# One ring of eight PSUM banks in place of three rings, and a new hand-fixed order of all items, in a delta-rule attention with a softplus MLP behind it

## The chip, the cores and the metric

The kernel runs on one core of a Trainium2 chip. The metric is the device time of one launch in microseconds (us); lower is better. Engines are named as the profile names them: PE (TensorE matmul), PEld (its weight load), DVE (VectorE), ACT (ScalarE), POOL (GpSimd) and SP (SyncE, here only a queue that issues DMAs).

## The reference

Batch 4, 8 heads, 768 steps, head size 48. Each of the 32 heads runs a delta rule over time; the rows of all heads are then the input of a two-layer MLP with softplus.

```
k_n = k / (norm(k) + 1e-6);  state = 0            # per head, 48 x 48
for t in range(768):
    y[t]  = g[t] * (q[t] @ state)
    state = state + beta[t] * outer(k_n[t], v[t] - k_n[t] @ state)
x = y, as 3072 tokens x 384
out = softplus(x @ w_in) @ w_out                  # 384 -> 2048 -> 384
```

Inputs and output are float32; the kernel computes its matmuls in float16 with float32 sums.

## The kernel before

Time is cut into 12 chunks of 64 steps. Per chunk the recurrence is turned into matrices: normed keys and queries are transposed on PE (`trs`, lines 422 and 454), their products are formed (`gram`, line 516) and copied out of PSUM with a sign (`kkc`) or a triangular mask (`mask`), and for each **pair of chunks** the inverse of a unit triangular matrix is built by forward substitution: 15 `step` items, each two small elementwise instructions (lines 664 and 671) on DVE or POOL, then `ca`/`cb` (masked copies), `st` (transposes on DVE) and the matmuls `xmm`, `tmm`, `zmm` (lines 744, 768, 789). Pair 0 is chunks 0 and 1, pair 1 is chunks 2 and 3, and so on.

The serial part is a **chain** per chunk: `ks` (keys times state, line 826), `w` (DVE), `umm` (880), `u1` (a copy out of PSUM), `zu` (893), `u2` (copy), `smm` (910), `s` (new state, DVE), which starts the next chunk's `ks`. Beside it `qs` (826 too) and `ymm` (936) make the output, `y` multiplies by g on DVE, `ytr` (963) transposes, and `xt` copies the result out.

The **dense** part takes `xt`: chunks 0, 1, 10 and 11 alone, the others in pairs. `g1` (line 989) is the first layer, one PSUM bank of 512 columns per item; `soft` (1001, ACT) applies softplus into one of 16 `ga` buffers; `g2` (1016) is the second layer in quarters of 4 matmuls, summed over four quarters in one bank; `o` copies the bank out and two `store` DMAs send it off. `dense` matmuls use the whole 128 x 128 array, `trs` and `ytr` too; all other matmuls are packed as tiles of 64 x 64 or smaller. `fill` items (line 1046) are matmuls whose result nobody reads; they run where the order has nothing else for PE.

Everything is recorded as numbered items, 1286 of them, and emitted in the order of the table `_ORDER`: a letter for the engine (P, A, D, G for POOL, S for SP) and the item's number. Each engine runs its own items in that order and waits only where data or a buffer demands it. An item that needs a new buffer takes the one that was given back longest ago in its ring:

```
for b in it.bufs:
    if b.ap is None:
        b.slot = b.ring.free.pop(0)
...
    b.users -= 1
    if b.users == 0:
        b.ring.free.append(b.slot)
```

So the table sets the order on each engine and which instruction must have read a bank before PE may write it again. In PSUM the rings are `p_d` (5 banks, everything of the recurrence), `p_h` (2 banks, `g1` and `fill`) and `p_o` (1 bank, `g2`). The inputs k, q, v and g come by 96 loads of 192 KB from SP into a ring of 12 buffers; `w_in` and `w_out` come in four pieces each from POOL's queue (`wload`, line 330).

Of the kernel before, what the change touches and what calls it, by code (L numbers as in the profile page):

```python
# [10 lines left out]
F32 = mybir.dt.float32  # L11
# [76 lines left out]
def kernel(  # L88
# [13 lines left out]
    P = 128  # L102
# [8 lines left out]
    G8 = C // 8  # L111
# [9 lines left out]
    def ring(name, n, shape, dt, where=pool):  # L121
        return Ring([where.tile(shape, dt, name=f"{name}{i}") for i in range(n)], name)
# [949 lines left out]
D244 D245 D248 D246 A293 D250 S23 S42 G273 A368 P369 S57 A370 S66 P145 P194 P136 P255 A247 A249 S31
S58 S17 D196 P264 D251 D195 S18 D257 A254 D256 G253 P258 A300 G8 D252 G121 D265 A260 P301 P135 G123
D294 S20 D266 S19 D274 G6 A259 P261 P716 A13 A295 A262 A263 A717 A718 P191 D192 A275 S21 P719 A720
S38 S37 D193 D302 D721 P147 A713 G122 D16 P219 S65 G315 G14 G361 G126 P725 D221 G125 D220 P722 D727
D726 G316 P728 D296 P137 D276 D297 D277 A724 A723 A729 P934 P928 A935 A929 D362 G363 P298 D299 P926
A927 S40 P278 D279 P303 A304 P308 A310 A309 P930 D306 D305 P283 A284 A285 P936 D307 D312 D364 P288
A931 D311 G365 D287 D292 P731 P932 A289 A290 A937 S39 D291 D286 D313 G124 P366 P267 A268 A269 G730
P150 P270 S67 S45 A933 D314 G317 G318 D733 A381 G319 G320 A367 D732 S46 D382 P735 A737 A736 D272
D271 P949 P950 D321 D322 G127 G323 P222 D224 P734 S68 D223 D324 D325 S73 P738 P938 A739 A740 P744  # L1080
A939 D326 D745 P940 G327 P371 P741 D746 D328 P747 G128 P164 S81 D742 A748 G329 A372 S99 D743 A941
G330 P951 D374 P970 A373 D331 P376 A388 P956 A971 G332 D379 D380 P749 D375 S74 G333 A378 D334 P958
A377 A957 D751 G383 A959 D336 P964 D338 A337 P389 S82 A335 P962 A390 D339 G342 P952 A965 S48 P343
D384 P352 S76 A341 D345 D344 G385 A953 D750 D340 P960 P346 A449 A348 S84 P942 A961 S47 A963 D347
D354 P753 A754 P349 A469 S75 P966 D450 D351 G451 A350 D755 D353 P968 S83 A967 P386 D470 S100 S98
D387 P752 P756 D758 P943 D757 G471 S53 D452 P391 A393 S54 P944 D392 A954 D395 P762 D394 D764 P396
A397 A955 P759 D760 A398 P945 D761 A946 D401 S97 P355 P972 G403 G453 A356 A969 P454 G476 S55 A357
P973 D763 A455 S56 P765 D402 G404 G405 D400 P974 A766 D399 G406 P767 A456 P358 D769 P975 G407 A360
D768 G408 P457 D359 A976 A978 S977 P770 G409 D458 G410 P771 A772 P979 S105 D773 A557 P477 D411 P774
G412 D775 A776 S62 P980 A564 D472 P780 S61 G413 A478 P777 D781 P981 D782 G414 A947 D473 P783 A784  # L1090
P459 P982 D460 D461 P992 A983 D462 D778 P474 S64 A993 P1008 D558 S92 A475 P1000 D779 A1009 P464 S89
D463 P479 A1001 P986 D468 A481 S113 D482 A466 D483 P990 D480 G415 G491 G416 G417 G418 G419 A987 D465
G420 P785 A991 D467 P988 D786 D787 P1012 G421 A989 S71 P484 G559 D424 A423 P998 S114 D422 A1013 D488
S90 D426 P1025 A485 A425 P996 P440 A486 D427 A999 P431 A997 S70 P994 G579 P1002 G645 S91 D489 A995
G430 P1004 A1003 S80 D433 A429 P1026 D432 G492 A1005 D490 G493 G494 P434 S106 A985 D428 S63 P1006
A436 A435 P1014 G495 D441 A1007 D442 P437 A1015 P789 S948 G496 G497 D438 P1010 A537 D790 D487 P1016
A439 D791 A1011 P1027 G498 D538 S69 A1017 P788 D560 P1028 G539 D499 P792 A1029 D500 P565 A793 D794
P1018 A566 D501 P795 D797 A1031 P798 P1019 G502 A1030 D800 D799 A625 P443 G561 P1020 D796 A444 D540
A445 G503 P801 P1021 D646 G504 P446 A1022 P803 D448 P1032 A802 S1024 G505 G506 D447 S72 D804 P562
S94 D805 P1033 A563 D626 P807 A809 D808 A544 P806 S79 P1034 G507 P810 P1035 A811 S115 D508 D509 D512  # L1100
A812 D511 P545 A1036 P816 A546 D510 P813 S78 D817 P1039 S107 G541 A513 D818 P572 A573 D815 P819 D576
S77 P1040 G647 A820 D575 D514 P542 A574 P1048 A543 P1060 D814 D580 A1049 D515 P547 P567 A1061 P1066
D551 A568 D550 G517 A569 D570 P1068 A1067 G518 S1037 D549 P552 G627 P1062 A1069 A548 S116 P1058 D556
D571 D554 D553 S85 A1063 D577 D578 P821 A1038 P519 P1052 A1059 P1072 S108 A1053 S86 S112 S96 P1041
A1073 P1056 A1057 D581 P1064 S87 G582 D521 G583 G584 P1042 D823 D822 A1065 P1050 D520 G585 D516
P1046 G586 A1051 P522 P528 D555 P1054 A523 D529 A524 A1047 D587 D628 P525 P825 A1043 S1045 D530 S95
P1074 D526 D588 G589 A826 P1085 S1044 A1055 P531 A527 P824 P1070 D827 D533 G590 G591 A1075 D532 D667
A632 P828 A829 P1076 D830 A1023 P1086 G592 A1077 P831 A1071 P834 D833 G629 G668 G593 P1087 D835 D836
# [24 lines left out]
"""

# [28 lines left out]
```

## Time and profile before

| | |
|---|---|
| time of three runs | 243.43, 243.91 (median), 245.13 us |
| span of the profiled execution | 241.5 us |
| what lies around the span | the page gives no other time for the profiled execution; the runs are 1.9 to 3.6 us above its span, the median 2.4 us |
| PE busy | 219.4 us (91%), 5020 matmuls |
| DVE, ACT, POOL busy | 161.7 us, 152.8 us, 113.7 us |
| first dense matmul | 40.51 us |
| first dense matmul of chunks 2 and 3 | 89.77 us |
| end of the last matmul | 237.56 us |

A row of the timeline reads: start, duration, engine, line, operation, written tile<-read tiles, shape, count, and in brackets the idle time before and what ended it. Durations of matmuls overlap, since they are pipelined; what a group costs PE is the distance from its start to the start of the next group. A row of the windows reads: from:to, length, then busy time and number of instructions of each engine, the granted PE clock (1.00 is full), and DMA share.

### The profile page before, as it was taken

How to read it: one execution, taken by the hardware profiler on the slowest of the kernel's cores; microseconds unless marked ns; L12 is line 12 of the kernel's file. 1: busy time of each engine (PE TensorE's matmuls, PEld its weight loads, DVE VectorE, ACT ScalarE, POOL GpSimd, SP SyncE). 2: the span in 40 equal slices, each digit the busy share in tenths (PEclk: the TensorE clock that was granted, in tenths of full speed). 3: DMA queues.
4: the chain of work that ended last, by engine and by line, in shares of the span. 5: the costliest groups of instructions: out<-in, count | busy, mean ns of one | idle time of the engine just before them, and what ended most of it. 6: DMA issues, size and time to landing. Idle time of an engine off the chain costs nothing.

```text
span 241.5 us, 11396 instructions
## 1 busy us (share of the span) xinstructions
PE 219.4 (91%) x5020; PEld 135.6 (56%) x5020; DVE 161.7 (67%) x368; ACT 152.8 (63%) x292; POOL 113.7 (47%) x197
## 2 busy tenths in 40 slices
PE   7645877879988999999999999999999999999983
PEld 2423455646764664556655566655565555677751
DVE  2768699888897889987899757896496310623000
ACT  5767576764982778876895767757363674143540
POOL 8740393875779778989597482016620000000000
PEclk9985599999999999999999999999999999999999
DMA  6999989999999399961889514962302311303112
GB/s 102 182 245 137 167 135 190 176 173 180 180 217 167 57 177 164 162 113 35 150 153 184 97 30 94 160 122 52 69 21 52 68 34 25 64 19 81 35 33 65
DMA packets 86833, 27.57 MB, mean 114 GB/s; under 512 B 77048, under 2 KB 86776, under 8 KB 86784
## 3 DMA queue, kind: packets, MB, share of 16 engines
q1 hardware_dynamic: 80624, 20.83, 52.6%
q0 software_dynamic: 3840, 3.17, 8.5%
q10 hardware_dynamic: 2320, 2.85, 5.2%
q8 instruction: 39, 0.64, 1.2%
q14 instruction: 10, 0.08, 0.1%
HBM read 25.26 MB, written 4.72 MB: 124 GB/s over the span
## 4 chain that ended last, share of the span: by engine, by line
PE 75%; DMA 7%; DVE 6%; SPq 4%; issue 3%; ACT 2%; POOL 1%; DVEq 0%; ACTq 0%; POOLq 0%
PE o L1016 27%; PE h L989 26%; DMA w_in<-in_moe_w_in_dram 4%; PE d L826 3%; SPq L305 3%; PE d L936 3%; PE d L516 2%; DMA f<-in_q_dram 2%; PE d L422 2%; PE d L963 2%; PE d L454 2%; PE d L880 2%; PE d L910 2%; PE d L893 2%; PE d L768 1%
## 5 line engine op out<-in xcount | busy, mean ns | idle before, releaser
L1016 PE MATMUL o<-w_out,ga 128*128 128x384 f16 x384 | 77.7, 327 | 0.7 <-ACT osb L209 0.6
L1001 ACT ACTIVATE ga<-h 128x512 f16<-128x512 f32 x96 | 56.5, 599 | 29.8 <-PE h L989 25.9
L989 PE MATMUL h<-xt,w_in 128*128 128x512 f16 (+1 forms) x384 | 74.0, 327 | 0.5 <-DMA w_in<-in_moe_w_in_dram 0.3
L989 PEld LDWEIGHTS <-w_in 128*128 128x128 f16 x384 | 34.5, 98 | 21.2 <-DMA w_in<-in_moe_w_in_dram 0.8
L1016 PEld LDWEIGHTS <-ga 128*128 128x128 f16 x384 | 33.7, 98 | 21.8 <-issue 0.8
L664 POOL TENSOR_TENSOR tmp<-nn,tt 128x78 f32<-128x78 f32 (+7 forms) x53 | 19.2, 362 | 16.1 <-DVE tt L671 13.0
L373 POOL TENSOR_TENSOR nv<-nv,half_c 128x16 f32<-128x16 f32 x8 | 23.5, 2940 | 6.6 <-DVE nv L362 6.5
L671 POOL TENSOR_TENSOR tt<-tt,tmp 128x78 f32<-128x78 f32 (+7 forms) x53 | 20.4, 385 | 4.2
L498 DVE TENSOR_TENSOR mt<-d,mask 128x256 f16<-128x256 f32 x48 | 18.2, 413 | 4.5 <-PE d L516 3.5
L209 ACT ACTIVATE kqt<-d 128x1024 f16<-128x1024 f16 (+1 forms) x18 | 18.0, 1000 | 4.8 <-PE d L454 3.6
L211 DVE CAST u<-d 128x384 f16<-128x384 f32 x20 | 10.9, 554 | 14.3 <-PE d L880 7.9
L209 ACT ACTIVATE u<-d 128x384 f16<-128x384 f32 x28 | 13.0, 490 | 11.8 <-PE d L880 5.4
L1046 PE MATMUL h<-ident 128*128 128x512 f16 x52 | 18.1, 493 | 1.7 <-DVE ident L197 1.7
L209 ACT ACTIVATE kk<-d 128x256 f16<-128x256 f32 x37 | 13.4, 386 | 6.3 <-PE d L516 5.4
L209 ACT ACTIVATE osb<-o 128x384 f32<-128x384 f32 x19 | 9.3, 492 | 9.4 <-PE o L1016 9.3
L454 PE MATMUL d<-ident,qn 128*128 128x128 f16 x96 | 8.5, 243 | 6.7 <-ACT qn L209 5.9
L950 DVE TENSOR_TENSOR yg<-d,f 128x384 f16<-128x384 f32 x24 | 12.3, 551 | 2.9 <-PE d L936 2.8
L924 DVE TENSOR_TENSOR s<-s,d 128x384 f16<-128x384 f16 x20 | 10.4, 542 | 5.7 <-PE d L910 4.3
L644 POOL TENSOR_TENSOR nn<-ln,beta_l 128x256 f32<-128x256 f16 x8 | 6.1, 780 | 14.2 <-DVE ln L627 14.2
L209 ACT ACTIVATE xt<-d 128x768 f16<-128x768 f16 x10 | 8.1, 813 | 7.0 <-PE d L963 7.0
L866 DVE TENSOR_TENSOR w<-f,d 128x384 f16<-128x384 f32 x22 | 11.3, 545 | 1.4 <-ACT xt L209 0.7
L362 DVE TENSOR_REDUCE nv<-f 128x16 f32<-128x768 f32 x12 | 11.3, 942 | 1.0 <-ACT f L351 1.0
(117 smaller groups left out, 346.7 us busy)
## 6 DMA issues: line engine op xcount, KB each, us to landing
f<-in_k_dram SPq DMA_DIRECT2D x24, 192.0 KB, 5.7
f<-in_q_dram SPq DMA_DIRECT2D x24, 192.0 KB, 5.6
f<-in_v_dram SPq DMA_DIRECT2D x24, 192.0 KB, 5.3
f<-in_g_dram SPq DMA_DIRECT2D x24, 192.0 KB, 5.3
out_dram<-osb ACTq DMA_DIRECT2D x29, 96.0 KB, 2.7
out_dram<-osb SPq DMA_DIRECT2D x19, 96.0 KB, 2.8
w_in<-in_moe_w_in_dram POOLq DMA_DIRECT2D x4, 384.0 KB, 7.9
w_out<-in_moe_w_out_dram POOLq DMA_DIRECT2D x4, 384.0 KB, 8.4
```

What stands on the lines that cost most here:

```text
L209: nc.scalar.activation(o, x, AF.Copy, scale=float(sign))
L362: lambda en: nc.vector.tensor_reduce(nvs().rearrange("p (a h) -> p a h", a=2), ksq.ap, mybir.AxisListType.X, ALU.add),
L373: nc.gpsimd.tensor_tensor(nvs(), nvs(), half_c[:, :NU], ALU.pow)
L454: nc.tensor.transpose(o[:, j], qn.ap[:, j].rearrange("p m d -> p (m d)"), ident)
L498: nc.vector.tensor_tensor(mt[c][m].ap[:, NP * p : NP * p + NP], gb[m].ap.rearrange("p (i b) -> p i b", i=NP)[:, :, n : n + C], mask[:, Non ...
L664: ENG[en].tensor_tensor(t, nn.ap[:, :, j : j + 1, j + 1 :].broadcast_to([P, 2, w, n]), tt.ap[:, :, :w, j : j + 1].broadcast_to([P, 2, w, n ...
L671: ENG[en].tensor_tensor(rows, rows, t, ALU.add)
L950: lambda en, m=m: nc.vector.tensor_tensor(heads(yg.ap, m), hd(yp[m].ap), heads(gf.ap, m), ALU.mult),
L989: nc.tensor.matmul(hp.ap[:, n * b : n * b + n], w_in[:, j, f * P : (f + 1) * P], xt.ap[:, j, t0 : t0 + n], start=(j == 0), stop=(j == 2),)
L1001: lambda en, hp=hp, o=gb: nc.scalar.activation(o.ap, hp.ap, AF.Softplus),
L1016: nc.tensor.matmul(op.ap[:, :DM], b.ap[:, col + c0 : col + c0 + 128], w_out[:, f, :], start=(f == 0), stop=(f == NF - 1),)
L1046: nc.tensor.matmul(hp.ap, ident, ident[:, None, :].broadcast_to([P, 4, P]))
```

## The change

The three PSUM rings become one ring of eight banks, used by `p_d`, `p_h` and `p_o` alike. The table is replaced as a whole: the order of all items, the engine of many of them (copies, steps, casts), and the number of fills in it (13 before, 11 now). A line that tied the second chunk pair's norms to the beta loads in the table's order is dropped; those loads still stand ahead of what reads them.

```diff
-    p_d = ring("d", 5, [P, 512], F32, psum)
-    p_h = ring("h", 2, [P, 512], F32, psum)
-    p_o = ring("o", 1, [P, 512], F32, psum)
+    p_d = p_h = p_o = ring("d", 8, [P, 512], F32, psum)
...
-    setup[2] += beta_it
...
-S26 S25 P138 P161 S33 S34 P151 A12 G4 S44 A173 S43 G2 A169 D176 P177 P174 D0 G227 A178 P188 D170 A15
+S26 S25 S34 S21 S33 P155 P143 P154 S19 S23 G6 G403 G5 G197 G2 D4 D3 D227 D173 G0 D176 A7 A1 A11 A15
...
```

Three lines fewer in the file put every later line of the code 3 lower (2 lower numbers between the rings and the dropped line): line 1016 becomes 1013.

**PE, middle of the program.** Each row is one instruction; `o0`, `d1`, `d5` are PSUM banks, `ga` the softplus results, L880 (now L877) is `umm`, L963 is `ytr`, L741 is `xmm`. Before, one quarter of `g2` stands between a 64-wide group and a transpose:

```order
L880 MATMUL d2_170<-w160_131,td1_126 64x48
L1016 LDWEIGHTS ga6_155
L1016 MATMUL o0_175<-w_out_73,ga6_155 128x384
L1016 LDWEIGHTS ga8_157
L1016 MATMUL o0_175<-w_out_73,ga8_157 128x384
L1016 LDWEIGHTS ga11_160
L1016 MATMUL o0_175<-w_out_73,ga11_160 128x384
L1016 LDWEIGHTS ga14_163
L1016 MATMUL o0_175<-w_out_73,ga14_163 128x384
L963 LDWEIGHTS yg0_145
```

Now two quarters of two output tiles, in two banks, often stand together; here is the seam between them and the next 64-wide group:

```order
L1013 MATMUL d1_169<-w_out_73,ga0_149 128x384
L1013 LDWEIGHTS ga14_163
L1013 MATMUL d5_173<-w_out_73,ga14_163 128x384
L1013 LDWEIGHTS ga8_157
L1013 MATMUL d5_173<-w_out_73,ga8_157 128x384
L1013 LDWEIGHTS ga5_154
L1013 MATMUL d5_173<-w_out_73,ga5_154 128x384
L1013 LDWEIGHTS ga4_153
L1013 MATMUL d5_173<-w_out_73,ga4_153 128x384
L741 LDWEIGHTS kk2_99
```

What moved: dense items stand in longer runs, and so do the 64-wide groups between them. Counted over the table, PE changes between whole-array and 64-wide (or narrower) work 170 times before and 130 times now.

**POOL, around the loads of the first layer's weights.** `kk` and `z` are copies of constants, `f` a square of k, `tx` a part of pair 0's inverse, `kn` the normed keys of chunks 2 and 3, `qn` a cast of q, `w` the first chunk's `w`. Before:

```order
L353 TENSOR_TENSOR f_75<-f_74 128x768
L211 COPY tx_123<-tb_122 64x512
L211 COPY kk_99<-pat 128x16x32
L330 DMA w_in<-in_moe_w_in_dram 128x3x512 x2
L211 COPY kk_98<-pat 128x16x32
L330 DMA w_in<-in_moe_w_in_dram 128x3x512
```

Now:

```order
L668 TENSOR_TENSOR tt_118<-tt_118,tmp_115 128x2x15
L403 TENSOR_TENSOR kn_88<-f_81,nv_93 128x16x48
L403 TENSOR_TENSOR kn_89<-f_74,nv_94 128x16x48
L209 CAST qn_90<-f_83 128x2x8x48
L855 TENSOR_TENSOR w_131<-f_79,nv_92 128x384
L855 TENSOR_TENSOR w_132<-f_79,nv_92 128x384
L327 DMA w_in<-in_moe_w_in_dram 128x3x512
L350 TENSOR_TENSOR f_85<-f_80 128x768
L327 DMA w_in<-in_moe_w_in_dram 128x3x512 x3
```

What moved: the weight loads now come after the last step of pair 0's inverse (L668; 8 of the 15 steps are on POOL now, 1 was), two key products, a cast and chunk 0's `w`.

**SP, start of the program.** Before, keys of chunks 0 and 1, then q of chunk 2 and v of chunk 0:

```order
L305 DMA f_74<-in_k_dram 64x16x48 x2
L305 DMA f_75<-in_k_dram 64x16x48 x2
L302 DMA f_76<-in_q_dram 128x1x384 x2
L305 DMA f_78<-in_v_dram 64x16x48 x2
L305 DMA f_79<-in_k_dram 64x16x48
L302 DMA f_81<-in_q_dram 128x1x384 x2
L302 DMA f_82<-in_q_dram 128x1x384 x2
```

Now beta loads stand between, q of chunks 0 and 1 come early, and v of chunk 0 is the 28th and 29th issue:

```order
L302 DMA f_74<-in_k_dram 64x16x48 x2
L302 DMA f_75<-in_k_dram 64x16x48
L262 DMA beta_l<-in_beta_dram 16x5x32
L302 DMA f_75<-in_k_dram 64x16x48
L262 DMA beta_l<-in_beta_dram 16x5x32 x2
L299 DMA f_77<-in_q_dram 128x1x384
L299 DMA f_78<-in_q_dram 128x1x384 x2
L299 DMA f_79<-in_q_dram 128x1x384 x2
L262 DMA beta_l<-in_beta_dram 16x5x32
L302 DMA f_81<-in_k_dram 64x16x48 x2
```

What moved: v of chunk 0 (7th and 8th issue before) went back behind k, q and beta. On the same queue 29 of the 48 output stores stand now, 19 before; ACT's queue has the other 19 (29 before).

More of the change, by code (lines that the diff above doesn't have):

```diff
@@ L1072 @@
[L1072 to L1108, printed above, removed]
@@ new lines @@
+A720 A304 S66 S65 S45 S46 D362 D315 G122 G363 G316 S73 S74 D307 D306 D730 P267 A269 P722 A723 A724
+A285 A268 P725 P288 P731 A289 D726 D727 D291 D732 D733 P270 P728 P734 A272 A729 A290 P735 A737 D292
+A736 P926 A927 A271 D311 D364 G365 D313 P934 A935 P928 P738 A740 P389 P936 A390 A937 S81 S82 D314
+D739 P744 D745 P741 D743 D746 S48 S47 G125 G317 G318 G319 G320 D321 G322 P366 P938 A367 A929 A939
+P371 P376 P747 A377 A372 A748 D742 P932 P940 A933 P962 P968 D379 D374 A969 P960 A963 A941 A961 P749
@@ new lines @@
+D413 D414 D415 G491 G492 P996 P1002 P986 D468 A995 A1007 P484 A997 A993 A1003 P479 D558 A480 A486
+A481 D485 P1008 D488 D487 D483 D482 D489 P1016 A1009 G416 G417 P1014 G418 G419 G420 G421 P1012 P998
+P988 P990 P1010 A987 A1015 A1017 P1000 P1004 A423 A422 A989 A991 A1011 A1001 A999 A1005 A1013 D424
+D425 D490 P1025 P785 D428 D426 D427 P431 D432 D430 D786 D433 P1018 P1026 P440 A429 P434 A435 A436
+D787 P1027 P788 D441 D442 P437 A439 D438 P789 A790 A537 P1028 D791 G559 G493 G494 G495 G496 G497
+G498 D560 D499 D500 D501 G579 G580 G502 G503 P443 P792 A445 A793 A794 A444 A1029 S108 S116 A544
@@ new lines @@
+D814 G645 G518 D646 S77 S96 P1072 A1073 A1065 P1054 P1046 P1070 A1071 P542 A1055 P1066 D543 P572
+P567 P1076 D576 A574 A569 A1047 A1067 P1052 D571 D573 A1077 D570 D575 D568 A1053 P1060 P519 D521
+D520 P547 P552 A549 A548 A1061 A554 D555 D550 D551 D517 D556 S95 S87 S94 P1062 P1068 A1063 A1069
+A553 P1058 P522 P528 D529 P821 A523 A524 A1059 D822 D530 D823 P1085 P1078 P525 P824 P825 P1079 P1086
+A1045 A827 P1099 P1080 D632 D527 D626 D826 D577 S80 S79 S88 S104 S1044 S101 S93 A526 P828 A830 A829
+P1081 P1100 A1082 A1023 P831 P834 P531 P1087 G647 D648 A1037 D578 D581 D582 D833 D832 A533 A532 P839
@@ new lines @@
+P534 D836 D835 A1038 A536 P633 D840 G627 D628 D841 P1101 P842 A634 P843 G667 G583 G584 G585 G586
+G587 G588 G668 D629 D589 D590 D591 D592 G593 G594 G595 G596 A844 A845 A535 P1102 S1084 A1103 S1105
+S120 S102 P1092 P846 P1088 P837 A848 A847 P852 P849 D838 D854 D853 P1093 P630 P855 P1094 P653 D1089
+G649 D851 D597 D601 D631 D850 A856 A598 A599 P1108 A654 A600 P1130 P1124 P1120 P1122 A1121 A1131
+A1109 P1128 A1129 A1123 P1106 P1095 P650 A1125 A651 P1112 S111 S110 D602 D604 D603 S103 S1090 S1091
+S117 S1104 G605 G606 D1096 A1113 P1126 A1127 A1107 P607 P857 D609 D608 D858 D859 P1110 A1111 P1136
@@ new lines @@
+P660 P655 A1137 P610 D658 D663 P1132 D659 D664 A662 A656 A611 A612 A1133 D661 D657 P1114 P635 P640
+P616 A1115 A641 A1083 D637 D617 D618 D643 D636 D639 D638 D644 P1116 P1118 P1138 A1117 A642 D665
+P1159 A1119 P861 P613 P860 A615 A862 D614 A863 P1139 P1160 P864 P619 P1140 A866 D865 D620 P867 D869
+P870 D871 D868 D621 P1134 A1135 D666 P1161 P875 P622 P1162 D877 D872 D876 G669 D624 D670 G671 D623
+P1141 P1145 D672 D673 D674 P879 P878 S1098 A881 A880 A1142 S1143 P1152 P1146 P882 G675 G676 P1153
+P873 A884 D883 D874 S112 S1144 P888 P885 D889 D890 D887 P1154 P1147 G677 G678 D679 P891 P1155 P1148
@@ new lines @@
+P903 D905 D904 P1222 P1198 A1223 A709 P1214 D907 D708 P710 P911 P1205 P909 P1215 P1206 A711 A910
+P1226 P1207 P1240 P1208 D712 D913 D912 D1216 A1217 A1227 A1209 A1224 P1230 P915 P914 A917 S1218 D916
+P1199 P918 P1234 P1200 D920 A919 P1228 P921 D923 D922 A1229 A1235 A1231 P1232 P1201 P1236 D1202
+S1203 S1204 P924 P1238 A1233 A1225 A1241 A925 A1239 P1242 P1249 P1256 P1243 P1260 P1262 A1261 A1237
+P1258 P1264 A1265 A1259 A1263 A1210 A1211 A1257 P1270 P1250 P1266 P1268 P1244 P1251 A1267 P1279
+P1272 P1252 P1245 P1273 P1280 P1274 D1253 A1255 A1269 P1281 S1254 A1271 P1275 P1282 D1246 A1248
@@ L1133 @@
+S1247 A1276 A1278 D1283 A1285 A1284 S1277
 """
```

57 lines of the change are left out of this document (29 added, 28 removed).

## The prediction

> **What bounds the kernel now.** The page first: which engine is full, and when.
>
> ```profile
> PE 219.4 (91%) x5020; PEld 135.6 (56%) x5020; DVE 161.7 (67%) x368; ACT 152.8 (63%) x292; POOL 113.7 (47%) x197
> PE   7645877879988999999999999999999999999983
> PEclk9985599999999999999999999999999999999999
> ```
>
> PE is full from slice 13 on and patchy before. Windows of the stages put numbers on that. The cuts are the first dense matmul (40.51), the first one of chunks 2 and 3 (89.77) and the end of the last matmul (237.56):
>
> ```profile
> 25.00:30.00 5.00, 5.00 (x52) 2.16 (x55) 3.11 (x6) 2.70 (x4) 1.82 (x2) 0.50 1.22 173
> 40.51:89.77 49.26, 44.62 (x1243) 31.76 (x1244) 42.61 (x91) 32.86 (x64) 36.53 (x52) 1.00 1.02 167
> 89.77:237.56 147.79, 147.03 (x3177) 88.63 (x3175) 89.52 (x193) 92.16 (x174) 55.58 (x106) 1.00 0.48 85
> 80.00:230.00 150.00, 149.78 (x3428) 91.07 (x3427) 97.64 (x211) 97.23 (x181) 62.60 (x121) 1.00 0.49 87
> ```
>
> So there are three stages. **A**, to 40.51: chunk 0 has to get through its inverse and chain before any dense work exists; PE mostly waits or runs fills. **B**, 49.26 us with 44.62 busy: PE has the dense work of chunks 0 and 1 to hide pair 1's inverse and chain, and is idle for 4.64. **C**, 147.79 us with 147.03 busy: pure PE time; only fewer or cheaper PE instructions shorten it. In C a single bank wait shows, among the waits of PE:
>
> ```profile
> PE o L1016 <- ACT osb L209: 0.6, 1, 0.6
> ```
>
> **C, worked out.** What does a change between whole-array and 64-wide work cost? Six neighbours from the timeline:
>
> ```profile
> 115.69 0.44 PE L880 MATMUL d<-w,td 64*64 64x48 f16 x32
> 115.97 0.45 PE L826 MATMUL d<-s,kqt 48*64 48x48 f16 x32
> 116.35 0.82 PE L1016 MATMUL o<-w_out,ga 128*128 128x384 f16 x4
> 117.10 0.44 PE L893 MATMUL d<-u,z 64*64 64x48 f16 x32
> 117.47 0.82 PE L1016 MATMUL o<-w_out,ga 128*128 128x384 f16 x4
> 118.13 0.61 PE L454 MATMUL d<-ident,qn 128*128 128x128 f16 x8
> 118.67 0.62 PE L936 MATMUL d<-u,mt 64*64 64x48 f16 x28
> ```
>
> From start to start, a 64-wide group costs 0.28 before another (115.69 to 115.97), and 0.38 and 0.37 before dense work. A quarter of `g2` costs 0.75 before a 64-wide group, 0.66 before a transpose. Each change costs about 0.10, either way. After the first dense matmul of chunks 2 and 3 the old table has 112 changes, the new one 78: 34 x 0.10 = 3.4 us less. One 64-wide group fewer is left there (81 for 82), 0.3, and one transpose item fewer, 0.54 - 0.10 = 0.4. The bank wait of 0.6 goes too, since output tiles now sit in several banks. What is late next there is ACT's copies between chain steps; the new order leaves less PE work over them (first rival), and I allow 1.0 us for that: the nearest row has 0.2 idle in 150 us, the other end is that rival. C becomes 147.8 - 3.4 - 0.3 - 0.4 - 0.6 + 1.0 = **144.1**.
>
> The last window's clock is 1.00, while three rings cycle through all eight banks. [...]
>
> **B, worked out.** Between the same two events the old table has 36 64-wide groups, 8 `trs`, 44 changes and 2 fills, the new one 27, 7, 31 and none. The fills' time:
>
> ```profile
> 40.51:237.56 197.05, 2.06 (x8) 0.66 (x8) 1.00 0.61 105
> ```
>
> Busy time falls by 9 x 0.3 + 0.4 + 13 x 0.10 + 2.06 = 6.5, to 38.1 us; the dense work is the same. What is missing was moved into A, beside waits. Idle time: `xmm` of pair 1 needs the inverse, which the old order gave at
>
> ```profile
> 66.00 0.69 PE L744 MATMUL d<-dn,kk 64*64 64x32 f16 x64
> ```
>
> and DVE's `ln` that opens it started at
>
> ```profile
> 47.48 1.93 DVE L604 STREAM_TRANSPOSE ln<-kk 128x1024 uint32<-128x1024 uint32 x1
> ```
>
> In the new order `ln` follows chunk 1's `w` on DVE, right at the first dense matmul, so about 47; its steps are 9 on DVE and 6 on POOL (7 and 8 before), with the last three pieces of `w_out` issued between them. From `ln` to `xmm` were 18.5 us, of which PE, then busy with dense work, took some at the end; so I expect the inverse through at 62 to 64. PE's work ahead of it (16 `g1` and 3 quarters of 0.65, 9 small items) is some 16 us and ends at 62.5. I take 2 us of idle time for all of B; the ends are 0 and the old order's 4.6.
>
> **A, worked out.** Pair 0's inverse opened with `nn` and closed with `ca`, nearly all on DVE, and the first dense matmul came 15.9 us after `ca` began, let go by a weight load:
>
> ```profile
> 14.97 0.73 DVE L644 TENSOR_TENSOR nn<-ln,bl 128x256 f32<-128x256 f16 x2
> 24.59 0.78 DVE L688 TENSOR_SCALAR ta<-tt,mx 128x256 f16<-128x256 f32 x2
> 31.69 8.77 DMA w_in<-in_moe_w_in_dram
> 40.51 1.49 PE h L989 x12
> 9.78 6.83 SPq L302 DMA_DIRECT2D f<-in_q_dram  x8
> f<-in_q_dram SPq DMA_DIRECT2D x24, 192.0 KB, 5.6
> 28.11 0.42 DVE L498 TENSOR_TENSOR mt<-d,mask 128x256 f16<-128x256 f32 x1 [1.63 <-PE d L516]
> 29.73 0.96 PE L744 MATMUL d<-dn,kk 64*64 64x32 f16 x64
> ```
>
> What a step costs on either engine, and POOL's items ahead of the weight loads now:
>
> ```profile
> L671 POOL TENSOR_TENSOR tt<-tt,tmp 128x78 f32<-128x78 f32 (+7 forms) x53 | 20.4, 385 | 4.2
> L664 POOL TENSOR_TENSOR tmp<-nn,tt 128x78 f32<-128x78 f32 (+7 forms) x53 | 19.2, 362 | 16.1 <-DVE tt L671 13.0
> L671 DVE TENSOR_TENSOR tt<-tt,tmp 128x120 f32<-128x120 f32 (+7 forms) x31 | 8.1, 261 | 1.1
> L664 DVE TENSOR_TENSOR tmp<-nn,tt 128x120 f32<-128x120 f32 (+7 forms) x31 | 8.0, 257 | 2.4 <-POOL tt L671 1.8
> L406 POOL TENSOR_TENSOR kn<-f,nv 128x768 f16<-128x768 f32 x6 | 8.9, 1476 | 3.2 <-PE d L910 2.4 <-DVE nv L383 0.7
> L858 POOL TENSOR_TENSOR w<-f,nv 128x384 f16<-128x384 f32 x2 | 1.6, 834 | 1.3 <-DVE bl L582 1.3
> ```
>
> The new order moves 7 more steps to POOL: 7 x (747 - 518 ns) = 1.6. It hands the inverse between the engines 6 times more, an estimate of 0.6. Step 0 now stands on POOL behind the cast of chunk 1's q, the 11th and 12th issue of SP at some 0.85 each (8 in 6.83), landing 5.6 later: near 17, so the steps open 3 later. Masks and reductions stand between the steps on DVE, mostly while POOL works: 1. So `ca` comes at 24.6 + 6.2 = 30.8. The 15.9 after it I keep: 12 more small items stand in it on PE, with their copies on ACT and DVE, but the old order lost some 3 us there: the transpose behind `ca` ended at 26.5, DVE then waited 1.63 for PE, and `xmm` came at 29.73 only, behind fills at half clock. First dense matmul: **46.5** (43 to 52). The weights: POOL ends its steps near 30, then 2 x 1.48 + 0.8 + 2 x 0.83 = 5.4; issue at 35.5, first piece 8.8 later at 44.3, the second, behind a square, near 46.5. Just in time. The dropped line costs nothing: the last beta load is SP's 33rd issue, near 28, and pair 1's first reader of beta stands on POOL behind `w_in`, past 38.
>
> **The sum.** 46.5 + 38.1 + 2 + 144.1 = 230.7 for the last matmul, against 237.56. Behind it:
>
> ```profile
> 237.59 0.49 ACT osb L209
> 238.11 0.50 ACTq L1035 DMA_DIRECT2D out_dram<-osb  x1
> ```
>
> The last tile's copy is on DVE now, and both its stores on ACT's queue, one behind the other, where one was on SP: 0.5 more. So 6.9 - 0.5 = 6.4 us less in the profiled execution, a span of 235.1. The median stands 2.4 above the old span: 243.9 - 6.4 = **237.5 us**.
>
> **Rivals.**
>
> 1. *The tight steps stall.* From `umm` to `zu` of chunks 2 to 11 the old order lays a median of 2.7 us of other PE work (items at the costs above), the new 1.5, and 1.1 at chunks 2, 4 and 11. Two copies on ACT take 0.87 and start after `umm` has drained:
>
> ```profile
> 52.73 0.87 ACT L209 ACTIVATE u<-d 128x384 f16<-128x384 f32 x2 [0.54 <-PE d L880]
> L1001 ACT ACTIVATE ga<-h 128x512 f16<-128x512 f32 x96 | 56.5, 599 | 29.8 <-PE h L989 25.9 <-PE o L1016 2.8
> ```
>
> With 0.44 of drain that is 1.3; with a softplus of 0.6 ahead, 1.9. So 0.2 to 0.8 is missing at half of ten chunks, and as much at other steps: 2 to 5 us, 239 to 242. For it: the chain is serial and its order is tighter. Against it: counted likewise, a bank is written again a median of 2.6 us after its last writer (2.3 before), and ACT gives 10 stores to SP. Chance 0.15.
>
> 2. *The clock falls in B.* After 3.9 us without work PE's clock went to half:
>
> ```profile
> 19.26 1.89 PE L454 MATMUL d<-ident,qn 128*128 128x128 f16 x16 [3.86 <-ACT qn L209]
> 20.94 1.91 PE L1046 MATMUL h<-ident 128*128 128x512 f16 x4
> 35.45 1.04 PE L1046 MATMUL h<-ident 128*128 128x512 f16 x4
> ```
>
> A fill took 1.91 for 1.04, until PE had worked without a break from 25 to 30. If the wait for pair 1's inverse (2 us in my sum) passes 3.9, it costs 2 more itself and half of some 4 us after it: 241.5. Chance 0.08. [...]
>
> 3. *A gets much longer, and the kernel slower.* POOL is one queue: `w_in` now waits behind chunk 0's `w`, which needs v, the 28th and 29th issue of SP. At 0.85 each it lands at 30; but single issues in the old trace stretched to 2.4:
>
> ```profile
> 7.33 2.41 SPq L305 DMA_DIRECT2D f<-in_k_dram  x1
> ```
>
> If v lands after 34, every us is a us for all that follows; 6.4 us more (v at 40, first dense matmul at 53) decides, and v at 44 gives 247. Chance 0.10, of which 0.07 over 1% slower.
>
> 4. *The ring does not matter.* PE's waits on banks sum to 0.6 us in C; if the new order's fewer changes are eaten by small waits too, 243.3. Chance 0.05.
> 5. [...] Chance 0.02; this is the rule named under C.
>
> **How the numbers follow.** The forecast has 0.60 (233 to 240), the rivals the rest. A measurement of this kernel can tell about 1% from no change. Faster by over 1% (under 241.5): 0.60 + 0.10 of the first + 0.06 of the second = 0.76. Slower: 0.07 of the third and 0.01 each of the last two = 0.09. Within: 0.15. The range: the low end has the first dense matmul at 43, no wait in B and none in C, 237.5 - 3.5 - 2 - 1 = 231, which asks for all three at once; two of them give 233. The high end takes in the first two rivals: 242.
>
> **What would show it.** First dense matmul near 46.5 with POOL's weight loads from 35.5; busy time of PE near 38 from there to the first dense matmul of chunks 2 and 3, at 86 to 87; from there 144 to the last matmul, with PE idle under 1.5. It is wrong if that second event is past 92, if stage C has over 4 us of idle time before `zu`, `smm` or `ks`, or if the clock row shows half speed after 50 us.

## The result: slower by 6%, and the profile after

The changed kernel takes **258.5 us** (median, 257.37 to 259.22) where the kernel before takes 243.87 beside it on the same chip: a ratio of **1.0605, 95% interval 1.0544 to 1.0666**. Forecast were 237.5 us and a range of 233 to 242. Most of the loss is time in which TensorE stood still because its next instructions had not come yet (waits of PE on "issue": 6.0 us in stage A, 1.3 in B, 5.1 in C); a smaller part is a copy that ran beside GpSimd (2.4 us). Line numbers of after are 3 lower than before's.

The page of after: the busy line, the 40 slices of PE and its clock, and the queue that brings instructions (packets, MB, share).

```profile
PE 219.7 (86%) x5012; PEld 141.1 (55%) x5012; DVE 175.6 (69%) x377; ACT 144.1 (56%) x291; POOL 114.6 (45%) x189
PE   7793683489979899986999898999999999999992
PEclk9977678559999999999799999999999999999999
q8 instruction: 39, 0.64, 1.0%
```

PE's busy time is the old one to 0.3 us, while the span grew from 241.5 to 255.4: all of the loss stands as idle time of PE, and the clock has a new hole at 45 to 57 us and a dip at 121 to 128. The same three stages by windows (columns as before: length, busy time of PE, PEld, DVE, ACT, POOL, then clock, DMA share, GB/s):

```profile
0.00:54.21 54.21, 34.32 (x859) 22.05 (x859) 38.24 (x88) 32.22 (x64) 32.10 (x55) 0.77 1.06 167
54.21:97.07 42.86, 38.70 (x1011) 28.29 (x1003) 35.27 (x73) 29.18 (x58) 30.42 (x40) 0.97 0.73 118
97.07:250.91 153.84, 146.63 (x3159) 90.80 (x3152) 101.54 (x216) 82.70 (x171) 52.03 (x95) 0.99 0.46 85
```

| stage | before | forecast | after |
|---|---|---|---|
| A, to the first dense matmul | 40.51 | 46.5 | 54.21 |
| B, to that of chunks 2 and 3 | 49.26 | 40.1 | 42.86 |
| C, to the last matmul | 147.79 | 144.1 | 153.84 |

Where does PE stand still? The timeline of PE in stage A answers it. These are the rows of `zu` of chunk 0 (L890) and of `ks` of chunk 1 (L823) there:

```profile
41.70 0.40 PE L890 MATMUL d<-u,z 64*64 64x48 f16 x26
44.59 0.30 PE L890 MATMUL d<-u,z 64*64 64x48 f16 x6 [2.49 <-issue]
47.72 0.35 PE L823 MATMUL d<-s,kqt 48*64 48x48 f16 x10
51.61 0.51 PE L823 MATMUL d<-s,kqt 48*64 48x48 f16 x22 [3.54 <-issue]
```

PE stops after 26 of 32 matmuls of one group, all of whose operands were ready when it began, and after 10 of 32 of another; "issue" says that it waited for nothing that the profile shows. In stage C, where before had no such row among the waits of PE (its two were in B, 0.8 and 0.6), the waits and one place of the timeline are:

```profile
PE d L907 <- issue: 2.7, 2, 2.4
PE d L786 <- issue: 1.9, 2, 1.1
PE d L823 <- issue: 0.5, 1, 0.5
```

```profile
117.70 0.30 PE L907 MATMUL d<-u,kn 64*64 64x48 f16 x14
120.40 0.34 PE L907 MATMUL d<-u,kn 64*64 64x48 f16 x18 [2.40 <-issue]
```

Queue q8 moves 39 packets of 16 KB, in before as in after. PE's stream is 10,024 loads and matmuls, 257 for each packet, so I read a packet as a block of 256 instructions of 64 bytes: an estimate from these two counts, and the bursts of experiment 6 do stop at every 256. A 64-wide group is 64 of these (32 weight loads, 32 matmuls) in 0.28 us; a dense item is 6 to 12 in 0.65. From the first stop to the second PE issues exactly 256 instructions, and in each stop a q8 packet is under way (42.06 for 1.09 us, 48.62 for 1.44) after whose end PE goes on 1.4 to 1.6 us later. Counted from the start of the program, two instructions for each matmul, all ten "issue" waits of PE in stages A, B and C stand 188 instructions behind a multiple of 256; the two of before stand at 190. The new order puts 14 groups of 64-wide work in a row into stage A (four of them `gram` items of 16 matmuls), where before's longest row had four. Into C it puts eleven stretches of three, eight of them of full groups, where the old one had none over two.

A second thing is new in A, on the way of pair 0's inverse. The forecast kept 15.9 us from `ca` to the first dense matmul, and with it `ca` on VectorE at the 0.78 us of before's row (L688 before, L685 now):

```profile
28.47 3.04 POOL L403 TENSOR_TENSOR kn<-f,nv 128x768 f16<-128x768 f32 x2
28.55 3.19 DVE L685 TENSOR_SCALAR ta<-tt,mx 128x256 f16<-128x256 f32 x2
L661 DVE TENSOR_TENSOR tmp<-nn,tt 128x126 f32<-128x126 f32 x9 | 2.6, 291 | 1.3 <-POOL tt L668 1.1
L661 DVE TENSOR_TENSOR tmp<-nn,tt 128x120 f32<-128x120 f32 x6 | 3.3, 546 | 0.1
```

The two `ca` took 3.19 us and ended with the two GpSimd products beside them. Among the steps of the inverse on VectorE it is rare: most take what they took before (291 ns for 289 at 128x126). Three of the 36 instructions of L661 took 1.40, 1.46 and 1.87 us, each beside a GpSimd square or key product; one of them makes the 546 of the second row, where before had 280.

### The profile page after: what moved, and what is told of

Same layout as the page of the kernel before. It is cut to its first block, busy times and chain, and to the rows that moved or that the text cites. A ratio compares the mean times of both kernels' runs of the same rounds, so it can differ in the third digit from the quotient of the medians.

```text
span 255.4 us, 11387 instructions
## 1 busy us (share of the span) xinstructions
PE 219.7 (86%) x5012; PEld 141.1 (55%) x5012; DVE 175.6 (69%) x377; ACT 144.1 (56%) x291; POOL 114.6 (45%) x189
## 3 DMA queue, kind: packets, MB, share of 16 engines
q10 hardware_dynamic: 1520, 1.87, 3.0%
## 4 chain that ended last, share of the span: by engine, by line
PE 40%; DVE 7%; ACT 4%; issue 3%; DVEq 0%; ACTq 0%
PE d L1013 19%; PE d L986 10%; PE d L823 2%; ACT ga L998 2%; PE d L933 2%; DVE mt L495 1%; PE d L890 1%; PE d L907 1%; PE d L786 1%; PE d L765 1%; PE d L877 1%; PE d L960 1%; ACT kqt L207 1%; PE d L741 1%; DVE ta L685 1%
## 5 line engine op out<-in xcount | busy, mean ns | idle before, releaser
L1013 PE MATMUL d<-w_out,ga 128*128 128x384 f16 x384 | 73.4, 330 | 1.3 <-DMA w_out<-in_moe_w_out_dram 1.2
L986 PE MATMUL d<-xt,w_in 128*128 128x512 f16 (+1 forms) x384 | 69.2, 330 | 0.4 <-issue 0.4
L998 ACT ACTIVATE ga<-d 128x512 f16<-128x512 f32 x96 | 51.6, 613 | 25.6 <-PE d L986 15.6
L661 POOL TENSOR_TENSOR tmp<-nn,tt 128x56 f32<-128x56 f32 (+7 forms) x48 | 16.8, 350 | 24.3 <-DVE tt L668 21.3
L668 POOL TENSOR_TENSOR tt<-tt,tmp 128x56 f32<-128x56 f32 (+7 forms) x48 | 18.2, 379 | 3.8
L661 DVE TENSOR_TENSOR tmp<-nn,tt 128x126 f32<-128x126 f32 (+7 forms) x36 | 13.5, 376 | 4.3 <-POOL tt L668 3.1
L1043 PE MATMUL d<-ident 128*128 128x512 f16 x44 | 15.0, 497 | 1.7 <-DVE ident L195 1.7
L403 POOL TENSOR_TENSOR kn<-f,nv 128x768 f16<-128x768 f32 x7 | 10.4, 1494 | 13.2 <-DVE nv L380 13.1
L823 PE MATMUL d<-s,kqt 48*64 48x48 f16 x704 | 11.7, 193 | 4.9 <-issue 4.4
L823 PEld LDWEIGHTS <-kqt 48*64 48x64 f16 x704 | 9.1, 113 | 8.3 <-issue 8.2
```

The lines of the kernel that those rows point to most:

```text
L661: ENG[en].tensor_tensor(t, nn.ap[:, :, j : j + 1, j + 1 :].broadcast_to([P, 2, w, n]), tt.ap[:, :, :w, j : j + 1].broadcast_to([P, 2, w, n ...
L668: ENG[en].tensor_tensor(rows, rows, t, ALU.add)
L823: nc.tensor.matmul(hd(o[m].ap)[HALF[r], pi], kq(c, r, pi)[FEAT[m], off : off + C], s0[r].ap[FEAT[m], pi], **start(pi),)
L986: nc.tensor.matmul(hp.ap[:, n * b : n * b + n], w_in[:, j, f * P : (f + 1) * P], xt.ap[:, j, t0 : t0 + n], start=(j == 0), stop=(j == 2),)
L998: lambda en, hp=hp, o=gb: nc.scalar.activation(o.ap, hp.ap, AF.Softplus),
L1013: nc.tensor.matmul(op.ap[:, :DM], b.ap[:, col + c0 : col + c0 + 128], w_out[:, f, :], start=(f == 0), stop=(f == NF - 1),)
```

## The experiments

**Theory F (fetching):** TensorE's instructions arrive in blocks of 256, and stretches of 64-wide groups run through them faster than they come. **Rival P (placement):** the new order makes PE wait for data, buffers or banks. **Rival R:** the one ring costs by itself. **Rival L:** it is the loads on the DMA engines that delay the fetch. ("After halved" and the like name the kernel that an experiment changes.)

### 1. The ring alone

```
-    p_d = ring("d", 5, [P, 512], F32, psum)
-    p_h = ring("h", 2, [P, 512], F32, psum)
-    p_o = ring("o", 1, [P, 512], F32, psum)
+    p_d = p_h = p_o = ring("d", 8, [P, 512], F32, psum)
-    setup[2] += beta_it
     (the order of before)
```

> The kernel before with its own order of items and only the three PSUM rings made one ring of eight. Theory of fetching (the time is lost where TensorE has run through its fetched instructions) and theory of placement (lost to waits that the new order makes) both expect no change, 243 to 245 us, PE busy 147 in stage C. The rival that the single ring costs waits by itself expects 247 us or more, with PE waiting for evictions (DVE or ACT d) in stage C.

Measured: 242.56 us, ratio 0.9952 (0.9902 to 1.0002). Its stage C:

```profile
90.14:236.85 146.71, 146.48 (x3178) 88.55 (x3175) 89.75 (x193) 92.12 (x174) 55.89 (x106) 1.00 0.47 85
```

R is out: if anything, the ring gains a little (experiment 9).

### 2. Which stage loses by itself

```
 _ORDER = items of before, up to its first g1 of chunks 2/3
+         then all others as they stand in after          (front_old)
 _ORDER = items of after, up to its first g1 of chunks 2/3
+         then all others as they stand in before         (back_old)
```

> The order of before up to the first dense matmul of chunks 2/3, and from there the order of after; one ring. If the 6.1 us that stage C lost are its own, the first 90 us stay as before and C takes about 154 us: 250 us. Theory of fetching: C again has 4 to 7 us of TensorE idle time with nothing to wait for, in the middle of 64-wide groups, but not at the same places, since blocks of 256 instructions now begin elsewhere. If C's loss only followed from the late start of stage B (loads that were pushed back), C takes 144 to 148 and the kernel 240 to 244 us.

> The order of after up to the first dense matmul of chunks 2/3, and from there the order of before; one ring. The first dense matmul then comes at 54 us and that of chunks 2/3 at 97 us as in after; stage C takes 148 us as in before: 251 us. If the long stalls of the front were a disturbance of one execution and not of the order, the first dense matmul comes at 47 to 48 us and the kernel takes 245 us.

`front_old`: 248.61 us, ratio 1.0204 (1.0146 to 1.0262). Its stage C by a window, and its longest wait there:

```profile
93.12:244.95 151.83, 146.18 (x3159) 90.45 (x3152) 100.63 (x213) 80.61 (x166) 49.77 (x89) 0.99 0.44 80
PE d L786 <- issue: 2.0, 1, 2.0
```

C is 5.1 us longer than that of `ring_only`, so C's loss comes with the new order of C also behind the old front. The profiled execution is the longest of the four (251.16), but the medians of the two kernels differ by 6.0 us too. The stop came behind the 19th of 32 matmuls of `zmm` 4; after stopped in the same group behind the 26th (0.81), and after's longest stop, in `smm` 4, is not there. F expected 4 to 7 us of such stops in C; only 2.3 of the 5.65 us idle are "issue", so here F explains less than half of the idle time. `back_old`: 275.42 us, far over the 251 that I expected. A is 53.13, so the loss of the front is reproduced, but C has one wait that neither kernel has:

```profile
118.06 2.72 PE L986 MATMUL d<-xt,w_in 128*128 128x512 f16 x6 [16.42 <-ACT ga L998]
```

ScalarE had stood for 15.5 us ahead of a cast of q. My splice had moved a load of q back in SP's queue, to an issue at 111.36, and the cast in ScalarE's queue kept the softplus behind it waiting. It says nothing on the old order of C; it shows what one late load costs in queues that run in order.

### 3. `ca` away from VectorE

```
-D246 D248     (ca 0.0, ca 0.1)
+A246 A248
```

> After, with the two ca instructions of pair 0 (1.6 us each beside GpSimd's kmul) moved from VectorE to ScalarE, where 64x256 to 128x256 copies take 0.4 us; nothing else changes. If VectorE is held up while GpSimd runs a product of two tiles, xmm of chunk 0 starts at 30.5 us instead of 32.9. The theory of fetching expects that little of these 2.4 us arrives at the first dense matmul, since the next block of instructions is late anyway: 53 to 54 us, the kernel at 257 to 258.5. If stage A is bound by its data alone, all 2.4 us arrive: 51.8 us and 256 us.

Measured: 257.07 us, ratio to before 1.0527 (1.0434 to 1.0620).

```profile
28.48 1.34 ACT L683 ACTIVATE ta<-tt,mx 128x256 f16<-128x256 f32 x2 [0.75 <-POOL tt L668]
31.01 0.43 PE L741 MATMUL d<-dn,kk 64*64 64x32 f16 x32 [1.57 <-DVE dn L711]
52.21 0.99 PE L986 MATMUL d<-xt,w_in 128*128 128x256 f16 x4
```

On ScalarE the two copies take 1.34 us beside the same GpSimd products, and `xmm` starts 1.9 us earlier than in after (31.01 for 32.90). The first dense matmul comes 2.0 us earlier (52.21 for 54.21): the gain arrived, and my expectation that F would swallow it missed. The two stops here sum to 5.55 us and those of after to 6.03, so up to 0.5 of the 2.0 may be theirs; each figure is from one profiled execution. PE again stopped after 26 of 32 in `zu` (2.56) and after 10 of 32 in `ks` (2.99): the stops moved along with the work (PE went on at 43.14 and 49.61, in after at 44.59 and 51.61), so a block's arrival follows PE's own progress and no fixed time.

### 4. Halved groups: fewer instructions, same order

```
-        for i in range(NP)          (zmm, umm, zu, ymm)
+        for i in range(NP // 2)
     likewise H // 2 for H in xmm, tmm, smm, ks, qs; one matmul on each bank at the start
```

> The kernel before with half of the matmuls left out of each 64-wide group except gram (16 instead of 32; every eviction, load and dense matmul stays; the output is wrong), and one matmul more on each bank at the start so that nothing unwritten is read. The control: stage C loses 0.14 us for each of some 70 groups, 147.8 to about 138 us; first dense matmul at 40 us as before.

> The same omission in after. The order, the waits on data and the chain of evictions stay, and TensorE has half as many instructions to fetch for its 64-wide groups. Theory of fetching: the stalls in the middle of groups go, stage C takes no longer than in the halved kernel before (134 to 138 us, where the whole kernels differ by 6.1 the other way), and the first dense matmul comes at 47 to 49 us instead of 54. Theory of placement: shorter groups hide less, so the same waits or longer ones stay, C takes 143 us or more, 5 us or more over the halved kernel before, and the first dense matmul comes at 53 us.

Measured once each: **after halved 240.26 us, before halved 243.81**. Stage C of before halved, then A and C of after halved:

```profile
90.78:238.19 147.41, 140.98 (x2042) 80.83 (x2039) 90.45 (x193) 91.94 (x174) 56.10 (x107) 0.98 0.48 84
```

```profile
0.00:47.97 47.97, 32.47 (x658) 19.93 (x659) 37.57 (x88) 31.74 (x64) 32.06 (x55) 0.85 0.99 168
89.46:233.76 144.30, 137.90 (x2024) 81.39 (x2016) 99.26 (x216) 82.71 (x171) 51.54 (x95) 0.99 0.49 89
```

With half the instructions to fetch, the new order is the faster one: A falls from 54.21 to 47.97, and C is 3.1 us shorter than in the halved old order, where it was 6.1 longer. (A falls also because its own groups are shorter; the halving doesn't separate the two.) Of PE's "issue" waits one is left, 0.3 us long. P expected C at 143 or more, which it is, but also 5 us longer than the control's, and A at 53; both of these failed, and P is out. F had the order of the two kernels and A (47 to 49) right, but not the time of C: 144.30 for 134 to 138. The control missed its number too: halved, before's C keeps 147.41, where I expected 138, since shorter groups cover less and PE is now idle for 6.4 us there; after's C has 6.4 too. So C's 3.1 us between the two are busy time alone (140.98 to 137.90).

### 5. Where the stops sit

```
             def fill(en, hp=hp, n=n):
                 ...
+            if n == 23:                       (the last fill ahead of xmm 0)
+                for i in range(64):
+                    nc.tensor.matmul(hp.ap[HALF[0], 8 * i : 8 * i + 8], ident[HALF[0], :64], ident[HALF[0], :8])
```

> After, with 64 tiny matmuls (64x64 by 64x8, 128 TensorE instructions) added to the last fill ahead of xmm 0, where TensorE waits 3 us anyway. Theory of fetching: the two long stalls of stage A sit at ends of blocks of 256 instructions, so they move 64 matmuls back in the order: from behind the 26th of 32 matmuls of zu 0 to behind the 10th of zmm 0, and from behind the 10th of ks 1 to behind the 26th of smm 0. If what stops TensorE belongs to zu and ks (their data, their banks), they stay behind the 26th of zu 0 and the 10th of ks 1. The time of A may go either way by 2 us.

The timeline of PE, rows of `zmm` of chunk 0 (L786) and `smm` of chunk 0 (L907):

```profile
39.85 0.28 PE L786 MATMUL d<-td,kk 64*64 64x32 f16 x10
42.78 0.36 PE L786 MATMUL d<-td,kk 64*64 64x32 f16 x22 [2.66 <-issue]
```

```profile
45.50 0.57 PE L907 MATMUL d<-u,kn 64*64 64x48 f16 x26 [0.56 <-ACT u L207]
49.25 0.31 PE L907 MATMUL d<-u,kn 64*64 64x48 f16 x6 [3.18 <-issue]
```

To the matmul as F said: behind the 10th of `zmm` 0 and the 26th of `smm` 0. `zu` 0 and `ks` 1 ran through. The stops belong to places in the instruction stream. The kernel took 259.31 us.

### 6. How fast instructions come

```
     prog.emit(_ORDER)
+    burst(20, ...); 24 loads of 192 KB into r_f tiles; burst(20, ...)    (tail_bursts)
+    burst(24, ...)                                                       (tail_quiet)
     (burst(n): n times the 32 matmuls of smm on two dead banks)
```

> The kernel before, with work added behind its last store: first 20 groups of 32 matmuls of 64x64 by 64x48 in a row (1280 TensorE instructions, five blocks of 256) with nothing to wait for and no transfers under way; then 24 loads of 192 KB into dead buffers, and the same 20 groups again as soon as the first tile of these has landed. If issue is the limit, both rows take 0.28 us a group, 5.6 us. Theory of fetching: the first row takes 2.5 to 3.5 us for each block after the first two, 9 to 14 us in all, with gaps in the middle of groups every 256 instructions; and the second row, whose blocks come through DMA engines that are full of loads, 5 us or more a block: 15 us or longer. If traffic has no part in it, both rows are equal.

> The kernel before with 24 groups of 32 64-wide matmuls (1536 TensorE instructions) in a row behind its last store and no load beside them. With loads beside it such a row went at 4.4 us for 256 instructions. If that is the fetch itself, the quiet row goes at 3.5 to 4.4 us for 256, 19 us or more in all; if the loads make most of it, at 2.5 us or less, 13 us in all; by issue alone at 1.1 us for 256, 6.7 us.

SP issued the loads of `tail_bursts` ahead of time, so both of its rows ran beside loads (DMA share 0.89 to 0.96 from 240 to 265). The first and the last but one of its full blocks, and those of the quiet row:

```profile
240.48 1.41 PE L1071 MATMUL d<-u,kn 64*64 64x48 f16 x128 [2.52 <-issue]
...
266.96 1.91 PE L1071 MATMUL d<-u,kn 64*64 64x48 f16 x128 [2.37 <-issue]
```

```profile
240.11 1.74 PE L1071 MATMUL d<-u,kn 64*64 64x48 f16 x128 [1.58 <-issue]
244.11 1.91 PE L1071 MATMUL d<-u,kn 64*64 64x48 f16 x128 [2.27 <-issue]
247.56 1.91 PE L1071 MATMUL d<-u,kn 64*64 64x48 f16 x128 [1.55 <-issue]
251.29 1.91 PE L1071 MATMUL d<-u,kn 64*64 64x48 f16 x128 [1.81 <-issue]
255.29 1.01 PE L1071 MATMUL d<-u,kn 64*64 64x48 f16 x61 [2.09 <-issue]
```

Every full row has 128 matmuls, 256 instructions, and then a stop. Beside loads a block takes (266.96 - 240.48) / 6 = **4.4 us** (I expected 5 or more), without (255.29 - 240.11) / 4 = **3.8 us**. Behind the first stop the clock was at half:

```profile
245.00:250.00 5.00, 2.93 (x206) 2.69 (x196) 0.00 (x0) 0.00 (x0) 0.00 (x0) 0.50 0.02 7
```

At that clock a row of 128 lasts 1.91 us; at full clock, at 0.28 a group, it would take 1.1 (an estimate from that price). So what was measured is a supply of 58 to 67 instructions per us beside half clock, where 64-wide work at full clock uses 230 (64 in 0.28 us); whether blocks come at another pace at full clock no run shows. In stage A of after, between the two stops, a block took 51.61 - 44.59 = 7.0 us, with the weight loads of `w_in` and loads of k and v under way at once. Most of the difference lies ahead of the packet: it started 4.0 us after the block before had begun (44.59 to 48.62), where it took 1.2 to 1.7 in the quiet row and 1.1 to 2.4 beside loads. Why it started late was not isolated.

### 7. Without the loads

```
         def fn(en):
+            if c >= 7:
+                return
             if name == "q":
```

> After, without the loads of q, k, v and g of chunks 7 to 11 (the buffers keep what they hold, so the output of these chunks is wrong); every other instruction is the same. Theory that loads delay the fetch: the stalls in the middle of 64-wide groups in stage C fall from 5.1 us to under 1.5, and C from 153.9 to 148 or less. If the runs of 64-wide groups alone outrun the fetch, the stalls stay at 4 to 6 us and C at 152 to 154.

> The same omission (loads of chunks 7 to 11) in the kernel before, as the control: stage C has nearly no stalls to lose, so both theories expect 147 to 148 us for it.

Stage C of after without these loads, and its longest stops:

```profile
100.17:252.71 152.54, 146.37 (x3160) 90.49 (x3152) 100.44 (x216) 83.08 (x171) 52.46 (x96) 0.99 0.21 42
PE d L788 <- issue: 1.8, 1, 1.8
PE d L909 <- issue: 1.1, 1, 1.1
```

The traffic of C halved (42 GB/s for 85), and the stops still sum to 3.9 us (5.1 with the loads) and C is 1.3 us shorter. The control, before without the same loads:

```profile
90.55:237.89 147.34, 146.63 (x3177) 88.45 (x3175) 89.46 (x193) 92.14 (x174) 55.77 (x106) 1.00 0.21 42
```

L is out as the cause in C: loads lengthen a fetch (4.4 for 3.8 us), but the stretches alone outrun it.

### 8. Dense work pulled in between

```
-xmm 5  tmm 4 | g2 | qs 4  zmm 4  umm 4 | g2 | tmm 5  zu 4 | g2  g2 | smm 4
+xmm 5 | g2 | tmm 4  qs 4 | g2  g2 | zmm 4 | g2 | umm 4  tmm 5 | g2  g2 | zu 4 | g2 | smm 4
     (and so on: 38 quarters moved, in C of front_old)
```

> As front_old (order of before until the first dense matmul of chunks 2/3, order of after from there), but in stage C a g2 or g1 quarter that comes later is put in front of a 64-wide group where more than two of these would follow each other, or where the last 256 TensorE instructions would take under 2.8 us: 38 quarters are moved, and the stage is back to 113 stretches. Theory of fetching: no long stall in the middle of a group is left, C 146 to 149 us and the kernel 243 to 245 us. Theory of placement (the chain's items stand where their data is late): the dense quarters only fill waits, or come before their softplus is done, and C stays at 151 or more, 248 us.

A miss: 255.41 us, ratio 1.0481 (1.0382 to 1.0580), slower than `front_old`. C at 151 or more is what P expected.

```profile
90.05:250.54 160.49, 149.35 (x3160) 90.01 (x3152) 100.23 (x213) 80.73 (x166) 49.20 (x89) 1.00 0.42 76
PE d L960 <- issue: 1.6, 1, 1.6
PE d L890 <- ACT z L207: 1.3, 1, 1.3
PE d L786 <- DVE td L209: 1.2, 1, 1.2
```

The stops in the middle of 64-wide groups are nearly gone, but the quarters that I pulled forward were the cover of later steps: 11 us of idle time, most of it now for evictions. These waits are not in after, so the run says little on what after waits for; it doesn't confirm F either. It does show the price of a change: C has 32 changes more than in `front_old` and after, and 3.2 and 2.7 us more busy time (149.35 for 146.18 and 146.63), 0.08 to 0.10 each.

### 9. A version that beats both, and the price of a change

```
 (ring_only, and in C:)
-umm 7 | g2 | gram 10.1 | g2 | qs 7
+umm 7  gram 10.1 | g2  g2 | qs 7
     and seven such moves; no stretch of more than three groups
```

> Ring_only (order of before, one ring of eight), with eight small moves in stage C by which a 64-wide group that stood alone joins another one or two across one to seven dense quarters: six groups moved earlier, one quarter moved ahead of zmm 9, zmm 11 moved later; 113 stretches become 97 and none has more than three groups, with at least one quarter of dense work between. If a change between the two kinds of work costs 0.10 us as counted in the prediction, C gets 1.6 us shorter than in ring_only (146.7): 145.1, and the kernel takes 241 us, ratio 0.99. If joining groups only trades the changes for waits for instructions or data, C stays at 146.5 to 148 and the ratio at 0.995 to 1.005.

> The single ring with the order of before, timed beside paired and the same runs of before: 0.995 if its first ratio was no accident, 1.00 if it was.

> If the 16 fewer changes are worth anything, this is faster than ring_only_again by 0.5% (1.2 us); if the single ring alone made paired faster than before, both ratios are equal.

`paired` first gave 240.55 us, ratio 0.9894 (0.9846 to 0.9942). Side by side with 12 runs each, `ring_only` has 242.25 us, **0.9952 (0.9916 to 0.9989)**, and `paired` 241.32 us, **0.9946 (0.9912 to 0.9980)**: the same. Stage C of the two:

```profile
87.96:235.18 147.22, 146.49 (x3177) 88.56 (x3175) 89.62 (x193) 92.26 (x174) 55.80 (x106) 1.00 0.48 85
```

```profile
88.55:235.08 146.53, 145.86 (x3178) 89.04 (x3175) 89.62 (x193) 91.76 (x174) 55.88 (x106) 1.00 0.47 85
```

16 fewer changes took 0.6 us of busy time, not 1.6. In the trace a short `gram` that joins two others saves 0.06 us (0.57 + 0.35 apart, 0.86 together): its 16 matmuls still add 0.29 there, 0.15 more than half of a 0.28 group. Both versions beat both kernels, by half a per cent and through the ring alone as far as these runs can tell.

## Why the prediction was wrong, point by point

The last matmul came 20.2 us later than forecast (250.91 for 230.7): 7.7 in A, 2.8 in B, 9.7 in C. The step that failed is the same in A and C: the sum charges PE only the time in which it issues (0.28 us for a 64-wide group) and waits only for data and banks. The runs show a third bound, the arrival of PE's instructions at 256 per 3.8 us or slower.

**A, where it failed first: "The 15.9 after it I keep".** The forecast had `ca` at 30.8 and the first dense matmul 15.9 us behind it. `ca` came at 28.55, earlier than forecast, and the dense matmul 25.7 us behind it. Of the 9.8 us too many, the two stops are 2.49 + 3.54 = 6.0 (`shift` moved them; halved groups, which have neither, bring A to 47.97), the delay of `ca` beside GpSimd 2.4 (moved to ScalarE, 2.0 came back, up to 0.5 of it from shorter stops), and the other 1.4 were not separated; the window of 45 to 55 us has the clock at 0.50, but after halved has that for part of it too. 54.21 - 6.0 - 2.0 = 46.2 is where the forecast had the event, though not for its reasons alone: `ca` itself was 2.2 us early (why was not tested; the forecast's 0.6 for handing the inverse over was an estimate that no run shows), and the 1.4 and what was left of the 2.4 made up for it. Two terms were missing from the sum, 6.0 and 2.4 us. POOL's weight loads were issued at 33.96 and from 36.23 on (35.5 in the forecast), and PE's waits in A have none for them, so the third rival, the only one with a much longer A, named the wrong mechanism.

**`ca` at 0.78 us.** The row was read in a place where GpSimd did nothing (idle for 9.52 us up to 26.91). In after the two copies took 3.19 us on VectorE beside two GpSimd products of 3.04, and on ScalarE, beside the same products, 1.34. What holds VectorE up there no run shows; beside GpSimd's 2.94 us of L373 (128x16) `ca` kept 0.44 in before.

**B was nearly right.** PE was busy 38.70 for a forecast of 38.1, and idle 4.2 for 2: 1.3 of "issue" and 1.2 for a load of `w_out` make the difference. The second event at 97.07 is late only by what A lost and these 2.8.

**C: the term that was missing is the supply; the price of a change held in part.** The allowance for stalls was 1.0 us, with 5 as the far end, and thought of evictions only. Measured start to start, the 39 stretches of 64-wide work in C take 37.0 us; at the undisturbed price that forecast and trace share (0.37 for a single group, 0.28 for each more, 0.14 less for a `gram` of 16) they would take 24.8. The 56 of before take 29.9 for 26.5. So fewer stretches saved 1.7 on this side, as counted, and 8.8 us were lost inside them: 6.0 in five stops between 0.5 and 2.6 us long (start to start; 5.1 as idle time), 0.8 in a stretch at half clock behind the longest, the rest in waits for data inside `xmm` and `gram`. The halved groups give the saving back: 3.1 us less busy time, for the 3.4 + 0.3 + 0.4 forecast. `spread` bears out 0.08 to 0.10 for a change; `paired`, with 0.6 for 16, shows that it doesn't hold for every one: neighbours in the trace gave it for full groups, and `gram` has its own.

**The fifth rival**, a clock that swings in C: its chance of 0.02, and the 0.01 of it among the slower outcomes, were an estimate that no run shows. What the runs show in its place: `ring_only` cycles all eight banks through everything at clock 1.00 in C, and where the clock fell in after, a stop stands ahead: 0.50 from 45 to 55 us, between and behind stops of 2.49 and 3.54, and 0.81 from 122 to 130, behind one of 2.40.

**Of the signs that it would be wrong two came**: the second event past 92 and half clock after 50 us. The third, over 4 us of idle time before `zu`, `smm` or `ks` in C, fell short: 3.2 there, 5.1 with the 1.9 of `zmm`, which it did not name. The rivals missed: none was that PE runs out of instructions. The two "issue" waits of 0.8 and 0.6 in before's B, both 190 behind a multiple of 256, were the same thing in small; the forecast doesn't mention them.

**The 2.4 us around the span** is a small error: in every execution that has both figures the time is 1.7 to 2.1 us above its span.

## What to carry to other kernels

Count instructions, not only microseconds: before pushing work with many small matmuls together, ask how many instructions stand in a row and whether 256 of them still take about 4 us (3.8 and 4.4 in the bursts here); a stop in the middle of a group with "issue" behind it, a multiple of 256 instructions from the next such stop, is the sign. An order that looks better by engine time can lose on supply (237.5 us forecast, 258.5 measured). Dense work between small groups may also give their instructions time to come: C of before, with 112 changes between the two kinds, has no such stop, that of after, with 78, has 5.1 us of them. A duration read beside an idle neighbour (GpSimd here) is no price for the same work beside a busy one: 0.39 us became 1.6.

## What the hardware showed that I had not expected

- In rows of 64-wide work TensorE's instructions came at 256 per 3.8 us without loads, 4.4 beside loads (both at half clock), and 7.0 in one case beside weight loads. The queue that the page calls `instruction` moved 39 packets of 16 KB for 10,024 loads and matmuls of PE, and with 64-wide groups the wait for a block was in sight: stops of 0.3 to 3.5 us in after.
- The stops lie to the matmul at a fixed count of instructions (188 behind multiples of 256 in after, 190 in before). When 128 instructions were put ahead, the stops came 64 matmuls earlier in the kernel's own work.
- A VectorE copy with a scalar operand went from 0.39 to 1.6 us beside a GpSimd product of two SBUF tiles; the transposes on VectorE beside the next GpSimd items, a cast and a product, took 1.07 and 1.04, where the one of before beside an idle GpSimd took 1.07.
